# Reordering the beginning of an adaLN + attention + ReGLU kernel: the norms, the first units and idle matmuls

## The chip, the cores and the metric

The kernel runs on one core of a Trainium2 chip. The metric is the device time of one launch in microseconds (us). TensorE is called PE here, its weight loads PEld, VectorE DVE, ScalarE ACT, GpSimd POOL, and the queue that issues most DMAs SP.

## The reference

One transformer block with adaptive layer norm on 2048 tokens of width 576, in float32:

```python
mod = (_silu(c) @ w_mod).reshape(c.shape[0], 6, 1, -1)
sa, ca, ga, sb, cb, gb = (mod[:, 0], mod[:, 1], mod[:, 2], mod[:, 3], mod[:, 4], mod[:, 5])
h = _layernorm(x) * (1 + ca) + sa
x = x + ga * A(h)     # A: q = h @ wq, 32 heads of 128; 16 kv heads from a cache, the last 512 keys;
                      #    softmax(q k^T / sqrt(128)) v, then @ wo
h = _layernorm(x) * (1 + cb) + sb
x = x + gb * B(h)     # B: ((gate > 0) * gate * up) @ W_down, gate = h @ W_gate, up = h @ W_up, F = 4608
```

## The kernel before

**Numbers in two parts.** A factor of an attention product is kept as a high part rounded to fp32r and a low part, the remainder (`split`, `hi`, `lo`). A product is three matmuls: high by high, weight's low by high, weight's high by low.

**Units.** Attention is cut into 128 units. A unit is one of 32 heads with one of four blocks of 512 tokens (`qb` 0 to 3). `VIS` lists which key/value group `g` (two heads) is visited with which blocks, and `UNITS` is the flat order. In before it starts with group 0 on blocks 0, 1, 2, 3, so units 0 and 1 use block 0, units 2 and 3 block 1, 4 and 5 block 2, 6 and 7 block 3; then group 1.

**One unit on the engines** (`u` is its number). PE makes the scores (`s_half`, 12 matmuls into two PSUM tiles `s`), the projection of the next unit (`qproj`, 14 matmuls, `qps`), the value product of the previous unit (`pv_half`, 12 matmuls in two halves) and pieces of the output projection (`wo`, 12 short matmuls). DVE takes the maximum of the scores (`t`), ACT and DVE split the projection (`qhi`, `qlo`), ACT exponentiates (`p`) and rounds (`hi`), POOL adds up (`ks`) and makes the low part (`lo`). The maximum crosses partitions in one of two ways. The `by_moves` way stays on DVE (`cross`). The other uses a small PE matmul with `quad` (`qm`, in `spread`), behind the next projection in PE's order. In the first `PE0` = 4 units (`by_pe`) the maximum is also subtracted on PE (`minus`, 4 matmuls).

**The norms.** Attention needs the normalized, modulated and transposed input `hT` of a block before the first projection of that block. `LayerNorm` does it in steps: `st` (statistics of one of four token tiles, DVE), `rs` (reciprocal root, POOL), `nm` (normalize a tile, ACT), `tr` (20 transposes on PE into PSUM, `lta`), `af` (scale and shift by the modulation columns `mcol`, then high and low part). The norm of block n for attention is called `a0` to `a3`. The columns come from `mod_step` (DVE adds up rows of `w_mod` scaled by silu(c), tiles `wmb`) and `mod_col` (PE sums over partitions, `mps`). `m2` and `gate_row` do the same for the gate `ga`, which scales `wo` on DVE before it is split.

**What sets the order.** Every engine runs its instructions in the order in which the Python code writes them. The unit loop calls `run(u, k)` between its parts, which emits all steps of the list `sched` that are due at time 10*u + k. `step(name, t, fn)` puts a step there; in before, `PLAN` shifts `t` by name. Steps with negative times come ahead of unit 0. Loads of weights (`rwA` for wq, `rkv` for keys or values, `roga` for wo) go through two buffers (`raw`); a buffer is free again when its low part is made. The SP queue issues loads in order, and a load whose buffer isn't free holds up those behind it. `keep` and `again` write split weights to DRAM and fetch them back for a second visit of a group.

## Time and profile before

| | |
|---|---|
| time, median of 3 runs | 2862.01 us (2859.11 to 2862.62) |
| the profiled execution | 2857.6 us, its span 2855.8 us |
| PE busy | 2815.0 us, 99% of the span |
| DVE, POOL, ACT busy | 79%, 74%, 52% |
| mean granted PE clock | 0.998 |

The profiled execution is 4.4 us below the median of the runs, and 1.8 us of it lie outside the span. The start of a unit is taken here as the start of its first score matmul (line 496). Units 0 to 8 begin at 35.42, 46.92, 60.74, 74.21, 92.26, 106.26, 122.33, 134.73 and 146.55 us of the span. From unit 7 on a unit takes some 11.85 us.

### The profile page before, as it was taken

The numbers are of one execution on the slowest core, as the hardware profiler recorded it, in microseconds if no ns is written. First come the engines' busy times: TensorE is split into PE (matmuls) and PEld (weight loads), VectorE is DVE, ScalarE is ACT, GpSimd is POOL, SyncE is SP. The second block draws the span as 40 slices with busy tenths as digits, with TensorE's granted clock in tenths as the row PEclk, the third lists the DMA queues.
The fourth block names the chain that finished last, engine by engine and source line by source line (L and its number), as shares of the span: only waits on it lengthen the run. The fifth ranks groups of instructions, "written<-read, shape, count | busy, mean of one in ns | idle before, by whom it ended". The sixth has DMA issues, their size and how long they took to land.

```text
span 2855.8 us, 41174 instructions
## 1 busy us (share of the span) xinstructions
PE 2815.0 (99%) x15006; PEld 2449.5 (86%) x15006; DVE 2246.8 (79%) x3384; ACT 1476.7 (52%) x2105; POOL 2123.8 (74%) x1564
## 2 busy tenths in 40 slices
PE   6999999999999999999999999999999999999999
PEld 5788888888888888888888888888888888888888
DVE  7899999999889998888889756676677466666666
ACT  5766666666766666666656444444444122222221
POOL 5688888888899989877778766788777356656653
PEclk9999999999999999999999999999999999999999
DMA  4012132222232213312243456666667844444442
GB/s 163 24 45 79 65 106 85 83 82 100 95 104 94 92 62 131 105 70 80 68 155 139 150 213 229 231 240 231 234 234 261 338 165 154 155 155 159 159 154 106
DMA packets 164506, 399.57 MB, mean 140 GB/s; under 512 B 15056, under 2 KB 62160, under 8 KB 164304
## 3 DMA queue, kind: packets, MB, share of 16 engines
q1 hardware_dynamic: 132912, 284.69, 29.9%
q10 hardware_dynamic: 31392, 112.26, 10.0%
q8 instruction: 118, 1.93, 0.3%
q14 instruction: 84, 0.69, 0.1%
HBM read 271.16 MB, written 154.57 MB: 149 GB/s over the span
## 4 chain that ended last, share of the span: by engine, by line
PE 83%; DVE 6%; POOL 5%; issue 2%; ACT 2%; DMA 2%; SPq 0%; ACTq 0%; DVEq 0%; POOLq 0%
PE gu L1016 26%; PE wo L660 12%; PE qps L424 11%; PE md L660 8%; PE st_P L1118 6%; PE s L498 3%; PE s L497 3%; PE s L496 3%; PE pv L635 3%; PE pv L634 3%; PE pv L633 3%; POOL lo L600 2%; DVE t L501 1%; DVE p L591 1%; POOL wop L795 1%
## 5 line engine op out<-in xcount | busy, mean ns | idle before, releaser
L600 POOL TENSOR_TENSOR lo<-p,hi 128x1024 fp32r<-128x1024 f32 x256 | 610.6, 2406 | 1.1 <-ACT hi L577 1.1
L609 POOL TENSOR_TENSOR ks<-ks,p 128x512 f32<-128x512 f32 x256 | 351.7, 1374 | 238.7 <-DVE ks L606 135.5
L501 DVE TRANSPOSE_TENSOR_REDUCE t<-s 128x32 f32<-128x1024 f32 x256 | 313.8, 1239 | 85.9 <-PE s L498 76.6
L1016 PE MATMUL gu<-hop_B,wop 128*128 128x512 f32 x1512 | 375.0, 391 | 0.2 <-POOL wop L795 0.2
L1016 PEld LDWEIGHTS gu<-hop_B,wop 128*128 128x128 f32 x1512 | 274.9, 188 | 51.1 <-POOL wop L795 0.9
L1016 PE MATMUL gu<-hop_T,wop 128*128 128x512 f32 x1260 | 316.1, 391 | 0.0
L424 PE MATMUL qps<-hTa,wA 128*128 128x512 f32 x1288 | 312.9, 394 | 3.1 <-DVE hTa L372 1.6
L660 PE MATMUL wo<-woga,ohi 128*128 128x288 f32 x1472 | 298.8, 295 | 2.0 <-POOL woga L183 1.4
L591 DVE TENSOR_TENSOR p<-s,mb 128x1024 f32<-128x1024 f32 x246 | 290.3, 1219 | 4.2
L424 PEld LDWEIGHTS qps<-hTa,wA 128*128 128x128 f32 x1288 | 244.5, 190 | 56.6 <-DVE hTa L372 3.2
L476 ACT ACTIVATE qhi<-qps 128x512 fp32r<-128x512 f32 x128 | 76.4, 597 | 366.9 <-PE qps L424 358.4
L660 PEld LDWEIGHTS wo<-woga,ohi 128*128 128x128 f32 x1472 | 245.9, 188 | 18.8 <-POOL woga L183 3.4
L1016 PEld LDWEIGHTS gu<-hop_T,wop 128*128 128x128 f32 x1260 | 227.8, 188 | 39.0
L577 ACT CAST hi<-p 128x1024 fp32r<-128x1024 f32 x256 | 259.5, 1042 | 1.5
L660 PE MATMUL md<-wogb,hhi 128*128 128x288 f32 x1272 | 256.9, 295 | 0.4 <-DVE acc L671 0.4
L593 ACT ACTIVATE p<-p 128x1024 f32<-128x1024 f32 x246 | 249.5, 1051 | 13.7 <-DVE p L591 13.4
L671 DVE TENSOR_TENSOR acc<-md,acc 128x576 f32<-128x576 f32 x159 | 119.9, 755 | 160.4 <-PE md L660 159.8
L660 PEld LDWEIGHTS md<-wogb,hhi 128*128 128x128 f32 x1272 | 210.9, 188 | 12.6 <-DVE acc L671 1.4
L1127 DVE TENSOR_TENSOR acc<-st_P,acc 128x576 f32<-128x576 f32 x160 | 121.1, 757 | 127.9 <-PE st_P L1118 127.9
L660 PE MATMUL wo<-woga,olo 128*128 128x288 f32 x736 | 217.8, 296 | 1.3 <-POOL olo L649 1.2
L660 PE MATMUL md<-wogb,hlo 128*128 128x288 f32 x636 | 187.5, 295 | 0.0
L649 POOL TENSOR_TENSOR olo<-rb,ohi 128x512 fp32r<-128x512 f32 x128 | 167.4, 1308 | 15.2 <-ACT ohi L645 15.0
(283 smaller groups left out, 7095.3 us busy)
## 6 DMA issues: line engine op xcount, KB each, us to landing
wop<-wk_P SPq DMA_DIRECT2D x133, 640.0 KB
wk_P<-wop ACTq DMA_DIRECT2D x119, 640.0 KB
wr<-wlay SPq DMA_DIRECT2D x68, 384.0 KB
rogb<-wd SPq DMA_DIRECT2D x68, 288.0 KB
againq<-akq SPq DMA_DIRECT2D x18, 640.0 KB
rwA<-wq SPq DMA_DIRECT2D x32, 320.0 KB
wlay<-wg SPq DMA_DIRECT2D x36, 256.0 KB
roga<-wo SPq DMA_DIRECT2D x32, 288.0 KB
```

The costliest lines, as they stand in the source:

```text
L424: return [lambda i=i, a=a, b=b: nc.tensor.matmul(ps, a, b, start=(i == 0), stop=(i == n - 1)) for i, (a, b) in enumerate(ops)]
L501: nc.vector.tensor_reduce(t5[u][:, 2 * h:2 * h + 2, :].rearrange("p k b -> p (k b)"), t.rearrange("p k (b j) -> p (k b) j", j=32), axis=AX ...
L577: nc.scalar.copy(hi_[u, h], pt[u, h])
L591: nc.vector.tensor_tensor(p, t, bc[u][:, None, :].to_broadcast([P, 2, 512]), op=ALU.subtract)
L593: nc.scalar.activation(p, p, AF.Exp, bias=0.0, scale=1.0)
L600: nc.gpsimd.tensor_sub(lo_[u, h], pt[u, h], hi_[u, h].bitcast(F32))
L609: nc.gpsimd.tensor_tensor(ks_[u], ks_[u], p[:, j, :], op=ALU.add)
L649: nc.gpsimd.tensor_sub(olo[u], o.pop(u), ohi[u].bitcast(F32))
L660: nc.tensor.matmul(ps[:, half, :H2], a[:, sl], w[b][:, cs], start=(n == 0 and seed is None), stop=(n == 5), skip_group_check=seed is not None)
L1016: nc.tensor.matmul(ps, a, c, start=s not in heir(m) and i == 0 and s not in seeds_of(m), stop=i == len(ops) - 1, skip_group_check=True)
L1118: nc.tensor.matmul(ps[:, j, :H2], x[:, sl], w[:, y, :], start=n == 0 and not second, stop=n == 2, skip_group_check=True)
L1127: nc.vector.tensor_tensor(t, ps[:, :, :H2], t, op=ALU.add)
```

## The change

- **Units.** `VIS` begins with group 0 on block 0, then group 1 on blocks 0 to 3, then group 0 on blocks 1 to 3. Block 0 so serves units 0 to 3, block 1 units 4 and 5, block 2 units 6 and 7, block 3 units 8 and 9. The weights of heads 2 and 3 and of group 1 are loaded ahead; those of group 0 are kept in DRAM and fetched again.
- **First norm.** `a0` is written out by hand. Its 512-wide parts are normalized before the tails, transposes go token tile by token tile, and `finish` takes high and low parts straight from the PSUM banks in an order given by `FIN0`. The sums for the two modulation columns lose the ACT and POOL help (`pre_scale`, `pre_add`), and the last rows of column 0 are added by PE.
- **Idle matmuls.** `warm` puts 22 matmuls whose result nobody reads between the first steps of PE.
- **Where steps go.** `PLAN` holds absolute times now, for norms, gate, loads, projections and stores. The projections of units 1 to 4 are steps of their own; that of unit 2 goes ahead of that of unit 1 and to another PSUM pool. The norms 2 to 4 and `m2` are spread over units 0 to 7.
- **Small ones.** Units 4 to 7 use `qm` on PE and not `cross` on DVE (`MOVE0` = 8). The first weights get their low parts on DVE. `c` is loaded through ACT's queue.

PE's rows ahead of the first projection, in before: the sum for column 1, the first transposes of `a0` (bank `lta`), the sum for column 0 (`mps`).

```order
L171 MATMUL mps_448<-ones,wmb_4_400 128x1 x5
L329 MATMUL lta_0_483<-ident,xna_0_459 128x128
L329 MATMUL lta_0_483<-ident,xna_1_462 128x128
L329 MATMUL lta_0_483<-ident,xna_2_465 128x128
L329 MATMUL lta_0_483<-ident,xna_3_468 128x128
L329 MATMUL lta_0_483<-ident,xna_0_459 128x128
L329 MATMUL lta_0_483<-ident,xna_1_462 128x128
L329 MATMUL lta_0_483<-ident,xna_2_465 128x128
L329 MATMUL lta_0_483<-ident,xna_3_468 128x128
L171 MATMUL mps_493<-ones,wmb_4_406 128x1 x5
```

The same place on PE now, with the idle matmuls (`warm`).

```order
L1420 MATMUL warm_462<-acc_126,ident 128x128 x4
L1420 MATMUL warm_467<-wmb_0_396,ident 128x128 x4
L358 MATMUL lta_0_472<-ident,xna_0_446 128x128 x2
L1420 MATMUL warm_475<-wmb_0_396,ident 128x128 x2
L358 MATMUL lta_0_472<-ident,xna_1_449 128x128 x2
L1420 MATMUL warm_480<-wmb_0_396,ident 128x128 x2
L358 MATMUL lta_0_472<-ident,xna_2_451 128x128 x2
L1420 MATMUL warm_485<-wmb_0_396,ident 128x128 x2
L185 MATMUL mps_488<-ones,wmb_4_400 128x1 x5
L358 MATMUL lta_0_472<-ident,xna_3_453 128x128 x2
L1420 MATMUL warm_498<-wmb_0_396,ident 128x128 x8
L181 MATMUL mps_513<-sT,wmb_4_406 128x1 x4
```

The transposes now stand token by token ahead of the column sums, with idle matmuls between them.

DVE's rows between the low part of the first projection (`qlo`) and the first maximum (`t`), in before. `lfa` and `hTa` numbered 2, 3, 8 and 1 here are those of block 1.

```order
L480 SCALAR_TENSOR_TENSOR qlo_595<-qps_566,qhi_593 128x512
L387 TENSOR_SCALAR lfa_2_637<-lta_2_0_623,mcol_454,mcol_499 128x512
L387 TENSOR_SCALAR lfa_3_639<-lta_2_1_628,mcol_454,mcol_499 128x512
L391 CAST hTa_2_633<-lfa_2_637 128x512
L391 CAST hTa_3_635<-lfa_3_639 128x512
L395 TENSOR_TENSOR hTa_7_636<-lfa_3_639,hTa_3_635 128x512
L391 CAST hTa_8_650<-lfa_4_651 128x512
L387 TENSOR_SCALAR lfa_1_661<-lta_0_614,mcol_454,mcol_499 128x512
L501 TENSOR_REDUCE t_0_674<-s_0_667 128x32
L501 TENSOR_REDUCE t_0_674<-s_1_676 128x32
```

The same place on DVE now, from the last low parts of block 0.

```order
L457 TENSOR_TENSOR hTa_4_552<-lfa_0_571,hTa_0_548 128x512
L457 TENSOR_TENSOR hTa_8_556<-lfa_4_566,hTa_8_556 64x512
L457 TENSOR_TENSOR hTa_6_554<-lfa_2_562,hTa_2_550 128x512
L136 TENSOR_SCALAR wmb_4_416<-wmb_0_412,sT 128x576
L306 BN_STATS sta_1_608<-acc_127 128x6 x2
L307 BN_AGGR mva_607<-sta_1_608 128x2
L557 SCALAR_TENSOR_TENSOR qlo_614<-qps_584,qhi_612 128x512
L139 SCALAR_TENSOR_TENSOR wmb_4_416<-wmb_0_412,sT,wmb_4_416 128x576
L578 TENSOR_REDUCE t_0_628<-s_0_621 128x32
L578 TENSOR_REDUCE t_0_628<-s_1_630 128x32
```

Block 1's high and low parts are gone from this place; one statistics step and two steps of `m2` stand there.

PE's rows of unit 1 in before, from its last score matmul to the value product of unit 0 (`pv`); `qps_775` is the projection of unit 2.

```order
L498 MATMUL s_1_761<-qlo_729,kv_0_559 128x512
L424 MATMUL qps_775<-hTa_0_655,wA_471 128x512 x2
L424 MATMUL qps_775<-hTa_1_657,wA_471 128x512 x2
L424 MATMUL qps_775<-hTa_2_633,wA_471 128x512 x2
L424 MATMUL qps_775<-hTa_3_635,wA_471 128x512 x2
L424 MATMUL qps_775<-hTa_8_650,wA_471 128x512 x2
L424 MATMUL qps_775<-hTa_4_656,wA_471 128x512
L424 MATMUL qps_775<-hTa_5_658,wA_471 128x512
L424 MATMUL qps_775<-hTa_6_634,wA_471 128x512
L424 MATMUL qps_775<-hTa_7_636,wA_471 128x512
L530 MATMUL qm_769<-t_1_759,quad 128x80
L633 MATMUL pv_815<-hi_0_722,kv_1_687 128x512
```

The same place on PE now.

```order
L575 MATMUL s_1_767<-qlo_728,kv_0_529 128x512
L607 MATMUL qm_778<-t_1_765,quad 128x80
L710 MATMUL pv_811<-hi_0_709,kv_1_734 128x512
L711 MATMUL pv_811<-hi_0_709,kv_1_734 128x512
L712 MATMUL pv_811<-lo_0_749,kv_1_734 128x512
L710 MATMUL pv_811<-hi_0_709,kv_1_734 128x512
L711 MATMUL pv_811<-hi_0_709,kv_1_734 128x512
L712 MATMUL pv_811<-lo_0_749,kv_1_734 128x512
L664 MATMUL s_0_758<-mr_797,minus 128x512 x2
L664 MATMUL s_1_767<-mr_797,minus 128x512 x2
L374 MATMUL lta_0_842<-ident,xna_0_775 128x128
```

No projection stands between the scores and `qm` in unit 1 any more (that of unit 2 went into unit 0), and block 1's first transposes come here.

```diff
+PLAN = {'wq2.c': -64, 'wq3.l': -64, 'v0.l': -50, 'wq3.c': 2.2, 'k1.l': -64, 'v0.c': 6, 'k1.c': 2.2, 'x2': 2.2,
...
+WARM = (4, 4, 2, 2, 2, 0, 8, 0)
+Q0 = "h3 h0 h1 h2 l0 l3 l1 b4 l2"
+QS = 5
+QW = [2]
+QLATE = [4, 8]
+FIN0 = "f3v h3v l3p h1a f2v f1a f4a h2v h0a l1p f0a l0v h4a l4v l2v"
+MOVE0 = 8
...
-    nc.sync.dma_start(cT, c)
+    nc.scalar.dma_start(cT, c)
...
     def by_moves(u):
-        return PE0 <= u < MOVES
+        return MOVE0 <= u < MOVES
...
-    VIS = [(g, (0, 1, 2, 3)) for g in range(HKV - NLAST)]
+    VIS = [(0, (0,)), (1, (0, 1, 2, 3)), (0, (1, 2, 3))]
+    VIS += [(g, (0, 1, 2, 3)) for g in range(2, HKV - NLAST)]
...
     def step(name, t, fn, *args):
-        sched.append((t + PLAN.get(name, 0), len(sched), fn, args))
+        sched.append((PLAN.get(name, t), len(sched), fn, args))
...
+        def finish(self, plan):
...
+            for op in plan.split():
+                d, e = int(op[1]), op[2]
...
+                if op[0] == "l":
+                    eng = nc.vector if e == "v" else nc.gpsimd
+                    eng.tensor_sub(lo, fs[d][p0:], hi.bitcast(F32)[p0:])
+                    continue
+                dst, a, m = hi if op[0] == "h" else fs[d], add[:, d:d + 1], mul[:, d:d + 1]
+                if e == "v":
+                    nc.vector.tensor_scalar(dst, self.ps[d], m, a, op0=ALU.mult, op1=ALU.add)
+                else:
+                    nc.scalar.activation(dst, self.ps[d], AF.Identity, bias=a, scale=m)
...
+    def warm(k, src):
+        if WARM[k]:
+            t = psM.tile([P, 512], F32, tag="mm", name=f"warm{k}")[:, :P]
+            for _ in range(WARM[k]):
+                nc.tensor.matmul(t, ident, src, start=True, stop=True)
...
+    for i in range(4):
+        first(ln0.stats, i)
+    first(ln0.rstd)
+    first(mod_step, 1, 0, big[1, 0])
+    first(mod_step, 1, 1, big[1, 1])
+    first(ln0.shift)
+    for part in range(2):
+        for i in range(4):
+            first(ln0.norm, i, part)
...
+    first(lambda: mods.update(a=(mc[0](), mc["one"])))
+    first(ln0.trans, (2, 3), psS, "s")
+    first(ln0.trans, (4,), psW, "w")
+    first(ln0.finish, FIN0)
...
+    step("wq1.l", -70, pq1[0])
+    step("wq2.l", -70, pq2[0])
+    step("wq1.c", -66, pq1[1])
     step("q0", -65, qproj, 0, 0, 14)
...
+    for v in range(1, QS):
+        step(f"q{v}.a", 10 * v - 9, qproj, v, 0, 9)
+        step(f"q{v}.b", 10 * v - 9, qproj, v, 9, 14)
```

More of the change, by code (lines that the diff above doesn't have):

```diff
@@ L165, in mod_col @@
         m = msum[j]
-        assert steps_done[j] == (3 if j == 1 else 5)
+        assert steps_done[j] == 5 - (j == 0)
+        ps = psM.tile([P, 512], F32, tag="mm", name=f"mps{j}")
+        if j == 0:
+            w = big[0, 4]
+            for t in range(5):
+                a = w[:64, t * P:(t + 1) * P] if t < 4 else big[0, 2][:64, 2 * D:1280]
+                nc.tensor.matmul(ps[:, 8 + t:9 + t], a, sT[:64, 4:5], start=True, stop=True)
         if j < 3:
             mod_pad(j)
-        ps = psM.tile([P, 512], F32, tag="mm", name=f"mps{j}")
         for t in range(5):
@@ L1282 @@
     pk0[0]()
+    load_mod(2, "wC")
     load_x(1)
@@ L1359 @@
-    step("wq1.l", -67, pq1[0])
-    step("v0.l", -66, pv0[0])
+            if key == "a":
+                step(f"{nm}.lo{k}", 23 if t_af[k] == 20.5 else 28 if t_af[k] == 25 and qb == 1 else t_af[k] + (1 if t_af[k] % 20 == 5 else 0), lambda ds=ds: ln.rest[ds]())
+    mc = {}
+    ln0 = LayerNorm(0, "a", [(hp, "hT", 512)] * 4)
+    t = iter(range(-400, 0))
+    def warm(k, src):
[3 more added lines that the diff above has]
+                nc.tensor.matmul(t, ident, src, start=True, stop=True)
@@ new lines, in first @@
+    def first(fn, *args):
+        step("start", next(t), fn, *args)
+    for i in range(4):
[7 more added lines that the diff above has]
+            first(ln0.norm, i, part)
+    for i in range(2, 5):
+        first(mod_step, 1, i, big[1, i])
+    first(warm, 0, acc[3][:, :P])
+    first(warm, 1, big[1, 0][:, :P])
+    for i in range(3):
+        first(ln0.trans, (0, 1), psS, "s", (i,))
+        first(warm, 2 + i, big[1, 0][:, :P])
@@ new lines, with tail @@
+    first(setd(mc, 1, lambda: mod_col(1, 1.0)))
+    first(warm, 5, big[1, 0][:, :P])
+    first(ln0.trans, (0, 1), psS, "s", (3,))
+    first(warm, 6, big[1, 0][:, :P])
+    for i in range(4):
+        first(mod_step, 0, i, big[0, i])
+    first(lambda: mc.update(one=mc[1]()))
+    def tail():
+        a = big[0, 4][:64, None, 512:D]
+        nc.gpsimd.tensor_copy(big[0, 2][:64, 2 * D:1280].rearrange("p (r n) -> p r n", r=2), a.to_broadcast([64, 2, 64]))
+    first(tail)
+    first(setd(mc, 0, lambda: mod_col(0, 0.0)))
@@ L1426 @@
         seen.add(g)
-    for i in range(1, first):
+    for i in range(1, HKV - NLAST):
         B = 80 * i
```

206 lines of the change are left out of this document (129 added, 77 removed).

## The prediction

> **What bounds the kernel now.** The page's first part says which engine sets the time.
>
> ```profile
> PE 2815.0 (99%) x15006; PEld 2449.5 (86%) x15006; DVE 2246.8 (79%) x3384; ACT 1476.7 (52%) x2105; POOL 2123.8 (74%) x1564
> ```
>
> PE is busy in all but 40.8 us of the span of 2855.8, so the question is where those lie. I cut the span where the first score matmul of each unit starts and asked for busy time by window (length, PE, PEld, DVE, ACT, POOL, then granted clock, DMA share, GB/s).
>
> ```profile
> 0.00:15.17 15.17, 0.00 (x0) 0.00 (x0) 10.49 (x30) 6.88 (x11) 4.25 (x13) 1.00 0.86 310
> 15.17:35.42 20.25, 17.73 (x74) 14.73 (x75) 14.05 (x30) 10.82 (x19) 10.99 (x10) 1.00 0.73 263
> 35.42:46.92 11.50, 7.94 (x35) 5.75 (x33) 10.70 (x18) 5.37 (x9) 7.04 (x6) 0.96 0.33 104
> 46.92:60.74 13.82, 12.87 (x44) 10.22 (x45) 10.74 (x27) 5.66 (x7) 8.18 (x6) 0.79 0.08 26
> 60.74:74.21 13.47, 12.52 (x62) 9.88 (x60) 12.00 (x20) 11.98 (x19) 10.86 (x8) 1.00 0.00 1
> 74.21:92.26 18.05, 14.86 (x68) 11.65 (x67) 16.40 (x35) 11.19 (x16) 11.68 (x9) 0.91 0.06 20
> 92.26:106.26 14.00, 13.62 (x76) 11.33 (x75) 12.00 (x23) 12.23 (x20) 10.02 (x8) 1.00 0.01 2
> 106.26:122.33 16.07, 14.17 (x74) 10.86 (x72) 12.47 (x22) 10.99 (x15) 10.07 (x6) 1.00 0.13 43
> 122.33:134.73 12.40, 12.11 (x65) 10.22 (x63) 12.09 (x22) 8.71 (x12) 9.85 (x6) 1.00 0.07 23
> 134.73:146.55 11.82, 11.82 (x64) 10.24 (x63) 10.52 (x20) 8.10 (x12) 10.09 (x7) 1.00 0.16 48
> 35.42:146.55 111.13, 99.91 (x471) 80.15 (x470) 96.92 (x178) 74.23 (x104) 77.79 (x54) 0.95 0.10 31
> 146.55:2855.80 2709.25, 2697.32 (x14466) 2354.62 (x14464) 2125.30 (x3149) 1384.74 (x1973) 2030.75 (x1489) 1.00 0.41 142
> ```
>
> Rows 3 to 10 are units 0 to 7. A unit is whole at 11.82 us, where PE never idles. From 146.55 on PE idles 11.93 us in 2709, and the change leaves that stretch as it is. What can be won lies ahead of it: the first 35.42 us, then 11.2 idle us in the eight units and a slow clock (0.04 of 11.50, 0.21 of 13.82 and 0.09 of 18.05, together 5.0 us). The end moves by as much as the start of unit 8, now 146.55.
>
> The chain of waits shows what unit 0 waited for (start, length, what):
>
> ```profile
> 25.31 1.70 POOL rsa L293
> ...
> 33.20 0.61 ACT qhi L476
> 33.83 0.69 DVE qlo L480
> 34.58 1.53 DVE lfa L387 x2
> ...
> 36.82 1.66 DVE hTa L395
> ...
> 39.54 2.30 DVE t L501 x2
> ...
> 42.44 0.45 PE qm L530 x2
> ...
> 43.60 0.72 DVE mb L566
> 44.34 0.63 ACT mr L569
> ```
>
> The first maximum (`t`) waits from 34.58 to 39.54 behind DVE's work for block 1.
>
> **Part 1: the first scores, 35.42 before.** These rows of the timeline carry it.
>
> ```profile
> 1.17 1.84 SPq L108 DMA_DIRECT2D acc<-x  x4
> 4.42 0.82 DVE L285 BATCH_NORM_STATS2 sta<-acc 128x6 f32<-128x288 f32 x2 [1.22 <-DMA acc<-x]
> ...
> 8.66 0.21 DVE L286 BATCH_NORM_AGGREGATE mva<-sta 128x2 f32<-128x12 f32 x1
> ...
> 9.28 1.04 POOL L293 TENSOR_TENSOR rsa<-rsa,mhalf 128x4 f32<-128x4 f32 x1
> ...
> 15.17 2.29 PE L171 MATMUL mps<-ones,wmb 128*128 128x1 f32 x10 [15.17 <-DVE wmb L1341]
> ...
> 26.77 5.46 PE L424 MATMUL qps<-hTa,wA 128*128 128x512 f32 x12 [1.13 <-DVE hTa L391]
> ...
> 33.00 2.67 PE L329 MATMUL lta<-ident,xna 128*128 128x128 f32 x20
> ...
> 36.53 1.40 POOL L395 TENSOR_TENSOR hTa<-lfa,hTa 128x512 fp32r<-128x512 f32 x1 [0.48 <-DVE hTa L391]
> ```
>
> And these of the groups by shape in the first 140 us (count, busy us, mean ns):
>
> ```profile
> L387 DVE TENSOR_SCALAR lfa<-lta,mcol,mcol 128x512 f32<-128x512 f32 x5 | 3.8, 794 | 0.1
> ...
> L130 DVE SCALAR_TENSOR_TENSOR wmb<-wmb,sT 128x576 f32<-128x576 f32 x3 | 2.5, 819 | 0.1
> ```
>
> - `c` leaves SP's queue, so x is issued 0.45 earlier: statistics end at 8.4, not 8.87. One small DVE step, then the root on POOL, 1.04 alone or 1.70 as at 25.31 beside DVE work. DVE runs `m1` beside it now, so I take 1.70: 10.4, and 10.65 with `shift`. ACT's first tile follows at 11.5.
> - DVE goes on alone: three `m1` steps, four `m0` steps and two pads, 6 x 0.82 and small ones, to 16.7. The two low parts of weights, 1.5, lie behind that, to 18.2, while PE works.
> - PE from 11.5: 8 transposes, 14 idle matmuls and 15 column matmuls. A column sum of five took 10 instructions, so each plain fp32 matmul is two: 8 + 28 + 30 = 66 instructions. Fast, an instruction of this kind takes 0.133 (20 in 2.67 at 33.00): 8.8. Slow, 0.229 (10 in 2.29 at 15.17): 15.1. I take fast, as 8 idle matmuls stand ahead: 20.3. The remaining 12 transposes, 1.6, bring the banks to 21.6.
> - `finish`: four DVE steps of 0.79, then three low parts of 0.69 (a `qlo` is the same size). ACT's six run beside it, POOL makes two. A DVE low part took 1.66 at 36.82 while POOL ran one from 36.53 to 37.93, so these queue: 0 to 1.4, I take 0.7. Sum: 21.6 + 3.2 + 2.1 + 0.7 = 27.6, and the last matmul follows at once.
> - `qhi` 0.61 is met by PE at 28.2; one statistics step (1.03) and `m2` stand before `qlo` on DVE, so the scores run freely from 29.0. That is 6.4 earlier than 35.42. ACT casts two more weights ahead of `qhi`, due at 25.5. With all that is issued before them they make 7.6 MB by the tiles' sizes; at the 310 GB/s of the window to 15.17 that is 24.5 us, and their buffers are free at 18.2, so they cost nothing, with one microsecond to spare.
>
> The Trainium skill ("SBUF — State Buffer", section "SBUF: two separate sides") says that a DVE instruction with two SBUF inputs and a POOL instruction hold one port pair in turn, each for its whole length. By that the 0.7 would be 1.4 and the time 0.7 more; the row at 36.82 agrees with the rule.
>
> **Part 2: units 0 to 7, 111.13 before.** A unit's work by rows of the chain:
>
> ```profile
> 58.60 0.93 PE s L587 x4
> ...
> 63.91 0.97 PE mps L151 x4
> ...
> 125.81 3.17 PE qps L424 x14
> 128.98 1.58 PE wo L660 x12
> ...
> 130.79 0.23 PE pv L634
> ```
>
> Twelve score or value matmuls are 2.73.
>
> - Unit 0, 11.50 before: 2.3 of scores, two projections 6.3, `qm` 0.45, `minus` 0.93. The maximum no longer waits for block 1, and its chain (2.30, 0.5, a statistics step, 0.45, 0.72, 0.63) lies under the projections: 10.1.
> - Unit 1, 13.82 before: scores 2.73, `qm`, value product 2.73, `minus`, 16 transposes 2.1, gate sum 0.97: 9.9. No projection covers the maximum any more: from the scores' end 2.30 + 0.5 + 0.7 for the sums + 0.45 + a statistics step 1.03 + 0.3 + 0.72 + 0.63, 6.6, against which only half a value product stands (and its low part waits for POOL, which has `ks` and a value split ahead). Then come half of `minus` 0.5, ACT's exponential 1.0 (it frees the score bank that the transposes need), 8 transposes 1.05, the other half of the value product 1.4, the gate sum 1.0, ACT's copy of it 0.8 and 8 transposes 1.05: 16.1, of it some 6 of waits. A slow clock can follow such a pause, as in before's row 46.92:60.74 (2.9 us): 0 to 2.9, I take 1.0. 17.1.
> - Unit 2, 13.47 before: 10.5 of work; its second score bank waits 1.4 for block 1's low parts on DVE, `qlo` another 1.0: 13.0.
> - Unit 3, 18.05 before: 11.6 and 1.1 behind ACT's exponentials: 12.7. Before waited here for block 2's high and low parts on DVE and ACT.
> - Units 4 and 6, 14.00 and 12.40 before: 11.85 + 20 transposes 2.67 + `qm` 0.45 each: 15.0.
> - Units 5 and 7, 16.07 and 11.82 before: 11.85 + 0.45 + 1.0, as the projection's last low parts come behind the maximum (2.30) on DVE: 13.3.
>
> Sum: 10.1 + 17.1 + 13.0 + 12.7 + 15.0 + 13.3 + 15.0 + 13.3 = 109.5, 1.6 less than 111.13. The norms' work moves into units that were full, so most of the second part is an exchange.
>
> Edits costed at nothing: the stores of group 0 (issued by ACT, hidden by its idle half), fetching it back from unit 7 on (three units ahead), POOL's tail copy (under `m0`). Without cover a store's issue costs a few tenths on ACT.
>
> **Sum.** 6.4 + 1.6 = 8.0: 2857.6 becomes 2849.6. The runs' median stands 4.4 above the profiled execution, so 2854.0 there.
>
> **The rivals.**
> - *PE stays slow until the first projection.* The 66 instructions take 15.1, not 8.8, and 12 transposes 1.2 more: 7.5 later, 0.5 left: 2861.5. For it: in before PE was nearly unbroken from 15.17, with transposes and column sums, and still took 0.455 a projection matmul (12 in 5.46 at 26.77, against 14 in 3.17). Against: the idle matmuls stream 128 columns each, more than a column sum. It decides if PE isn't fast by about 16 us. The Trainium skill ("TensorE: Matmul & The Clock Gate", section "Part 1: The HAM clock gate (the "warmup" mystery)") says that some 3.4 us of sustained activity open the clock. By that before would have been fast by 20, and the row at 26.77 doesn't show it; with it this rival falls and my sum stands. Chance 0.15.
> - *It comes out slower: ACT stands behind a store.* The split of the fourth query weight (`wq3`) takes the buffer of the first, which ACT's own queue is storing to DRAM; ACT's cast waits for that store, and behind it stand the key cast and unit 0's `mr`, due near 36. Landing by 35 costs nothing, each us later is one us; landing 22 us after its issue at 29 loses 16, the 8.0 and 8.0 more: 2870. Against: the loads ahead are small and the row 35.42:46.92 moves only 104 GB/s. Chance 0.08.
> - *Waits of units 1 and 2 are shorter and nothing collides at the start*: first scores run freely from 27, units 1 and 2 take 3 us less: 13 us, 2849. For it: DVE's statistics steps in unit 1's chain (1.03 each) can fall into time in which DVE waits for PE, and I added each in full. Against: the sums over `p` and the value split queue on POOL in the same stretch. Chance 0.20.
>
> **How the numbers follow.** My forecast has 0.57, and holds 2850 to 2859 (its unknowns: 1.4 at the port, 2.9 of clock, 1 to 2 of waits). 0.2% is 5.7 us, about what a measurement of this kernel can tell from no change. Faster by that means below 2856.3: 0.47 of the forecast's 0.57 and the third rival's 0.20, 0.67. Same: 0.10 of the forecast, 0.13 of the slow clock, 0.02 of the store, 0.25. Slower: 0.02 of the slow clock, 0.06 of the store, 0.08. The range reaches from 2845 (the third rival with 4 us more) to 2861, the greater part of the slow clock's case left out.
>
> **What would show it.** Right: scores of unit 0 between 27 and 30; transposes at 0.13 from 12 on; PE idle some 6 us in unit 1; units 4 and 6 near 15; unit 8 near 139. Wrong: instructions of 0.23 between 12 and 20; ACT idle ahead of the cast of `wA` behind a DMA; unit 8 after 146; a unit after the eighth that differs from 11.85.

## The result and the profile after

The changed kernel takes 2866.96 us (median of 21 runs, 2861.68 to 2872.55) against 2858.44 for the kernel before (21 runs, 2855.06 to 2862.62): 1.0029 times as long, 95% interval 1.0022 to 1.0035. The forecast was 8.0 us faster; it is 8.5 slower. The profiled execution took 2869.27 us, 11.7 above that of before, its span 2867.5. Before's median over 21 runs lies 0.8 above its profiled execution, not 4.4 as over the three runs that the forecast had; the forecast difference of 8.0 doesn't hang on that.

The first part of the changed kernel's page, busy time by engine:

```profile
PE 2822.0 (98%) x15068; PEld 2453.9 (86%) x15068; DVE 2262.1 (79%) x3380; ACT 1473.9 (51%) x2099; POOL 2109.9 (74%) x1554
```

Busy time by window in the changed kernel, cut at the first score matmul of units 0 to 8 and of unit 127, the last one (columns as in the prediction):

```profile
0.00:28.68 28.68, 17.50 (x109) 14.63 (x109) 22.36 (x50) 13.47 (x21) 6.78 (x13) 1.00 0.96 317
28.68:41.11 12.43, 11.09 (x46) 8.36 (x47) 11.40 (x25) 3.94 (x6) 5.39 (x5) 1.00 0.66 231
41.11:62.38 21.27, 14.55 (x51) 9.75 (x50) 19.66 (x37) 13.81 (x22) 15.46 (x12) 0.76 0.18 59
62.38:75.44 13.06, 10.91 (x52) 8.51 (x51) 12.89 (x22) 7.74 (x12) 8.23 (x8) 1.00 0.13 35
75.44:90.98 15.54, 12.32 (x58) 9.38 (x56) 14.33 (x23) 8.85 (x13) 10.33 (x7) 1.00 0.20 70
90.98:105.85 14.87, 14.44 (x87) 12.60 (x85) 13.73 (x22) 13.14 (x20) 12.32 (x8) 1.00 0.51 179
105.85:119.20 13.35, 12.83 (x67) 10.41 (x66) 12.65 (x21) 9.01 (x14) 9.33 (x9) 1.00 0.20 72
119.20:135.31 16.11, 14.64 (x86) 12.59 (x85) 13.23 (x21) 13.86 (x20) 12.17 (x8) 1.00 0.00 1
135.31:148.27 12.96, 12.42 (x67) 10.54 (x66) 12.09 (x20) 7.29 (x10) 4.98 (x3) 1.00 0.18 54
148.27:1581.18 1432.91, 1427.29 (x7482) 1236.50 (x7481) 1295.99 (x2171) 953.53 (x1302) 1202.87 (x739) 1.00 0.29 93
1581.18:2867.50 1286.32, 1273.97 (x6986) 1120.59 (x6984) 833.80 (x979) 429.30 (x667) 822.07 (x747) 1.00 0.57 197
```

The same last two stretches in the kernel before:

```profile
146.56:1579.87 1433.31, 1427.32 (x7482) 1236.50 (x7481) 1296.94 (x2171) 955.71 (x1307) 1207.81 (x742) 1.00 0.28 92
1579.87:2855.80 1275.93, 1269.99 (x6986) 1118.11 (x6984) 828.35 (x980) 429.02 (x667) 822.93 (x747) 1.00 0.56 199
```

Unit 0 begins at 28.68, 6.7 earlier than before and nearly where the forecast had it. The eight units then take 119.6, where the forecast had 109.5 and before 111.1, so unit 8 begins at 148.27, 1.7 later than before. (Executions of one and the same program text differ here too: in `b_swap` and `b_noS3`, which are the kernel before as far as unit 127, unit 8 begins at 146.98 and 147.86.) Units 8 to 126 are alike (1432.91 against 1433.31). The stretch from unit 127 to the end, with the last unit and the MLP, takes 10.4 longer, with the same number of PE instructions: PE idles 12.35 in place of 5.94 and is busy 4.0 longer. There are two places to explain, then: units 0 to 3, and that last stretch. Unit 8 was forecast at 138.5, so 9.7 of the profiled execution's miss lie ahead of it, and 10.4 behind the start of unit 127.

**Units 0 to 3.** The chain of waits of the changed kernel in unit 1 (start, length, what):

```profile
49.40 0.06 DVE rr L641
49.48 2.29 DVE rr L642
51.80 0.72 DVE mb L643
52.55 0.63 ACT mr L646
53.22 1.24 PE s L664 x2
```

And POOL's timeline at that place:

```profile
47.05 4.69 POOL L677 TENSOR_TENSOR lo<-p,hi 128x1024 fp32r<-128x1024 f32 x2
```

`rr` splits a 128x16 column of maxima into two parts so that PE can subtract it (`minus`). Its second step takes 2.29 and ends when POOL's two `lo` end, at 51.74. All instructions that write `rr`, by line (count, ns min/median/max, first and last start), in the changed kernel:

```profile
L641 DVE CAST rr<-t x5: 121/546/1285, 36.2 to 1588.1; 128x16 fp32r<-128x16 f32 x5
L642 DVE TENSOR_TENSOR rr<-t,rr x5: 176/177/2311, 37.3 to 1589.4; 128x16 fp32r<-128x16 f32 x5
```

and in the kernel before:

```profile
L564 DVE CAST rr<-qm x5: 113/114/176, 43.2 to 1586.9; 128x16 fp32r<-128x16 f32 x5
L565 DVE TENSOR_TENSOR rr<-qm,rr x5: 174/174/175, 43.4 to 1587.0; 128x16 fp32r<-128x16 f32 x5
```

The input is `t` now, a tile in SBUF, where it was `qm`, a bank of PSUM. That comes from one line of `max_bc` that neither my excerpt of the diff nor my list of costs had:

```diff
-        r = bps[u][:, 256:272] if by_pe(u) else t5[u][:, 0, :]
+        r = t5[u][:, 0, :]
```

It holds for the units in which PE subtracts the maximum: 0 to 3, and the last one, 127, where the cast took 1.28 for 0.11.

PE's wait isn't all of it. The granted clock in the changed kernel's unit 1 is 0.76 over 21.27, 5.1 us lost by the forecast's way of counting. With the old line (`a_psum` below) it is 0.90, 1.7 lost; PE idles 1.6 less in that unit and is busy 2.6 less, with the same instructions:

```profile
42.99:60.07 17.08, 11.95 (x51) 8.21 (x50) 16.33 (x36) 13.76 (x22) 13.10 (x11) 0.90 0.20 65
```

**The last stretch.** DVE's timeline in the MLP of the changed kernel:

```profile
1911.29 6.07 DVE L900 TENSOR_TENSOR wr<-wr,wr 128x768 f32<-128x768 f32 x1
1917.28 0.75 DVE L748 TENSOR_TENSOR acc<-md,acc 128x576 f32<-128x576 f32 x1
```

POOL's at the same time:

```profile
1910.99 0.97 POOL L871 TENSOR_TENSOR wop<-wr,wop 32x256 fp32r<-32x256 f32 x1 [1.83 <-ACT wop L870]
1911.93 1.29 POOL L872 TENSOR_TENSOR wop<-wr,wop 128x512 fp32r<-128x512 f32 x1
1913.19 1.43 POOL L201 TENSOR_TENSOR wogb<-rogb,wogb 128x576 fp32r<-128x576 f32 x1
1914.58 1.28 POOL L1233 TENSOR_TENSOR hlo<-c,hhi 128x512 fp32r<-128x512 f32 x1
1915.83 0.71 POOL L871 TENSOR_TENSOR wop<-wr,wop 32x256 fp32r<-32x256 f32 x1
1916.51 1.97 POOL L872 TENSOR_TENSOR wop<-wr,wop 128x512 fp32r<-128x512 f32 x1
```

And PE's:

```profile
1918.08 0.53 PE L737 MATMUL md<-wogb,hhi 128*128 128x288 f32 x2 [2.41 <-DVE acc L748]
```

`wr<-wr,wr` is one of four sums of weight tiles that DVE makes for the MLP; the code calls it `S3`. It begins at 1911.29, when POOL has just begun a row of instructions without a gap, and it ends 0.8 after the fifth of them, at 1917.36; the sixth takes 1.97 where its like took 1.29. Behind `S3` on DVE stands `acc`, which empties the bank of the down projection that PE wants next: PE waits 2.41. `S3` is made 17 times. In the changed kernel 15 of these take some 0.95 and two 6.07 and 6.08 (at 1911.29 and 1985.71); in the kernel before none:

```profile
L823 DVE TENSOR_TENSOR wr<-wr,wr x17: 944/947/953, 1621.4 to 2191.9; 128x768 f32<-128x768 f32 x17
```

```profile
L900 DVE TENSOR_TENSOR wr<-wr,wr x17: 944/947/6080, 1625.0 to 2203.1; 128x768 f32<-128x768 f32 x17
```

No line of that code is changed. What is changed is when DVE and POOL come there relative to each other: in the kernel before POOL runs nothing when `S3` begins, 17 times out of 17.

The 4.0 by which PE is busy longer are in the main a slow clock again, 3.0 more lost than in before. There are two such stretches, one behind the last unit's `rr` and one behind the first long `S3`; behind the second long one the clock stays at 1.00:

```profile
1591.80:1595.30 3.50, 3.50 (x15) 3.23 (x14) 1.29 (x2) 3.44 (x5) 1.31 (x2) 0.51 0.02 6
1919.50:1923.00 3.50, 3.50 (x12) 2.83 (x11) 0.76 (x1) 0.83 (x1) 3.06 (x3) 0.51 0.95 335
```

With 4.9 more of waits for `acc`, 0.9 for `mr` in the last unit and 0.6 for a late weight, that makes 9.4 of the 10.4.

### The profile page after: what moved, and what is told of

It reads as the page before. It is cut to its first block, busy times and chain, and to the rows that moved or that the text cites. A ratio compares the mean times of both kernels' runs of the same rounds, so it can differ in the third digit from the quotient of the medians.

```text
span 2867.5 us, 41282 instructions
## 1 busy us (share of the span) xinstructions
PE 2822.0 (98%) x15068; PEld 2453.9 (86%) x15068; DVE 2262.1 (79%) x3380; ACT 1473.9 (51%) x2099; POOL 2109.9 (74%) x1554
## 4 chain that ended last, share of the span: by engine, by line
PE 81%; DVE 6%; POOL 6%; DMA 3%; ACT 2%; issue 2%; SPq 0%; ACTq 0%; POOLq 0%; DVEq 0%
PE gu L1093 24%; PE wo L737 12%; PE qps L499 11%; PE md L737 6%; PE st_P L1195 6%; PE s L575 3%; PE s L574 3%; PE s L573 3%; PE pv L712 3%; PE pv L711 3%; PE pv L710 3%; POOL lo L677 2%; POOL wop L872 1%; DVE t L578 1%; DVE ws L900 1%
## 5 line engine op out<-in xcount | busy, mean ns | idle before, releaser
L499 PE MATMUL qps<-hTa,wA 128*128 128x512 f32 x1190 | 284.4, 389 | 0.5 <-DVE hTa L417 0.5
L737 PE MATMUL wo<-woga,ohi 128*128 128x288 f32 x1376 | 279.7, 295 | 1.1 <-POOL woga L201 0.7
L499 PEld LDWEIGHTS qps<-hTa,wA 128*128 128x128 f32 x1190 | 223.2, 188 | 47.3 <-DVE hTa L417 0.9
L737 PEld LDWEIGHTS wo<-woga,ohi 128*128 128x128 f32 x1376 | 229.8, 188 | 16.1 <-POOL woga L201 2.9
L737 PE MATMUL wo<-woga,olo 128*128 128x288 f32 x688 | 203.6, 296 | 1.3 <-POOL olo L726 1.0
```

The costliest lines, as they stand in the source:

```text
L499: return [lambda i=i, a=a, b=b: nc.tensor.matmul(ps, a, b, start=(i == 0), stop=(i == n - 1)) for i, (a, b) in enumerate(ops)]
L737: nc.tensor.matmul(ps[:, half, :H2], a[:, sl], w[b][:, cs], start=(n == 0 and seed is None), stop=(n == 5), skip_group_check=seed is not None)
```

## The experiments

Sixteen kernels; "a" stands on the changed kernel, "b" on the kernel before. All times are medians, with the ratio to the kernel before in the same measurement (its median in brackets). Unit 8, unit 127 and the rest from there come from the profiled execution, as does the number of `S3` that took over 5 us; "rest" is the stretch from unit 127 to the end.

| kernel | us (before) | ratio, 95% | unit 8 | unit 127 | rest | long `S3` |
|---|---|---|---|---|---|---|
| before | 2858.44 | | 146.56 | 1579.87 | 1275.93 | 0 |
| after | 2866.96 (2858.44) | 1.0029, 1.0022 to 1.0035 | 148.27 | 1581.18 | 1286.32 | 2 |
| a_last | 2863.38 (2858.96) | 1.0016, 1.0007 to 1.0025 | 148.16 | 1580.82 | 1277.28 | 0 |
| a_psum | 2857.36 (2858.96) | 0.9995, 0.9986 to 1.0003 | 143.38 | 1576.05 | 1280.55 | 1 |
| b_last | 2860.93 (2858.96) | 1.0007, 0.9998 to 1.0016 | 147.77 | 1580.60 | 1278.5 | 0 |
| b_sbuf | 2862.12 (2858.96) | 1.0014, 1.0005 to 1.0023 | 150.56 | 1583.66 | 1279.9 | 1 |
| a_late | 2859.01 (2859.12) | 1.0001, 0.9992 to 1.0009 | 144.95 | 1577.89 | 1280.1 | 1 |
| a_nowarm | 2861.14 (2859.12) | 1.0008, 0.9999 to 1.0017 | 145.17 | 1578.01 | 1281.6 | 2 |
| a_both | 2857.41 (2859.24) | 0.9990, 0.9981 to 0.9999 | 141.97 | 1574.60 | 1281.80 | 1 |
| b_start | 2866.32 (2859.24) | 1.0027, 1.0016 to 1.0038 | 148.63 | 1581.79 | 1282.3 | 1 |
| a_swap | 2872.76 (2859.12) | 1.0048, 1.0036 to 1.0061 | 144.62 | 1577.06 | 1293.9 | 4 |
| b_swap | 2873.24 (2859.12) | 1.0053, 1.0041 to 1.0066 | 146.98 | 1579.90 | 1291.1 | 5 |
| a_c | 2859.06 (2858.39) | 0.9999, 0.9990 to 1.0008 | 139.69 | 1571.81 | 1287.19 | 2 |
| b_cq | 2861.26 (2858.39) | 1.0008, 0.9999 to 1.0018 | 148.10 | 1581.1 | 1279.2 | 1 |
| a_noS3 | 2852.41 (2859.21) | 0.9978, 0.9969 to 0.9986 | 141.38 | 1574.25 | 1277.15 | left out |
| b_noS3 | 2857.69 (2859.21) | 0.9999, 0.9991 to 1.0008 | 147.86 | 1580.62 | 1276.28 | left out |
| a_s3late | 2855.30 (2859.21) | 0.9988, 0.9979 to 0.9997 | 140.47 | 1573.19 | 1279.31 | 0 |
| a_s3early | 2859.42 (2859.21) | 1.0004, 0.9995 to 1.0012 | 140.42 | 1573.77 | 1284.7 | 2 |

### The column of maxima

The theory: the one line costs what is missing in units 0 to 3 and part of the end. The rival: the moved steps themselves cost it, and the place of the column is nothing. `a_psum` puts the old line back, `a_last` only for the last unit; `b_sbuf` puts the new line into the kernel before, `b_last` only for the last unit.

```diff
 a_psum:
-        r = t5[u][:, 0, :]
+        r = bps[u][:, 256:272] if by_pe(u) else t5[u][:, 0, :]
 a_last: the same with "if u == NU - 1"
 b_sbuf:
-        r = bps[u][:, 256:272] if by_pe(u) else t5[u][:, 0, :]
+        r = t5[u][:, 0, :]
 b_last: the old line with "if u < PE0"
```

> The changed kernel with the column in PSUM in units 0 to 3 and in 127, the old line. Port theory: in unit 1 the subtraction into rr, 2.28 us beside POOL's lo, takes 0.2; the pause on PE shortens by 2.1 us and the slow clock behind it by some tenths to 2 us, so unit 8 starts 2 to 4 us earlier than 148.27 and the median lies 2 to 4 us under a_last's. Rival: something else ends as late in unit 1 (the low parts on POOL), unit 8 starts within 0.5 us of 148.3 and the median equals a_last's.

> The changed kernel, but in the last attention unit (127) the column of maxima stays in PSUM as in before. Port theory: the cast to rr there, 128x16, took 1.28 us against 0.11 because its input now lies in SBUF and POOL runs lo beside it; it comes back to 0.11 and the start of the MLP stage moves from +3.5 to about +1.3 us. Carry-over theory: the 8 us lost later in the MLP stage (two weight sums held 6.1 us each) follow from that late start, so the median falls to 2857 to 2861. Rival, independent: the MLP stage loses its 8 us whatever the last unit does, and only 2.2 us go: about 2864.7.

> The kernel before with the column in SBUF in units 0 to 3 and in 127. Port theory: units 0 to 3 lose 0 to 4 us beside b_last, wherever POOL happens to run at the rr steps, rr steps over 0.5 us show it. Rival: the same time as b_last, since the projection covers the step in these units.

> The kernel before, with only the last unit's column of maxima in SBUF. Port theory: the cast to rr of unit 127 takes some 1.2 us, and the MLP stage starts about 2.2 us later. Carry-over theory: the MLP stage loses 5 to 8 us more, median 2865 to 2868. Independent: 2.2 us alone, about 2860.6.

The instructions that write `rr` in `a_psum`, by line:

```profile
L641 DVE CAST rr<-qm x5: 111/113/174, 38.4 to 1583.0; 128x16 fp32r<-128x16 f32 x5
L642 DVE TENSOR_TENSOR rr<-qm,rr x5: 174/174/176, 38.6 to 1583.2; 128x16 fp32r<-128x16 f32 x5
```

The waits are gone from all five units, and the median falls by 9.6 against the changed kernel's (0.0034 of the ratio). `a_last` alone gains 3.6, which leaves the other 6.0 for units 0 to 3. `a_last`'s profiled execution, 2859.88, is the lowest of its 11 runs, so its rest of 1277.28 is better than its usual one. In the kernel before the same line costs 3.2 (`b_sbuf`) and 2.0 for the last unit alone, whose interval includes no change. It costs in units 0 to 3 there too: PE waits 6.4 for `mr` in `b_sbuf` and 2.1 in `b_last`, and unit 8 begins 2.8 later. That the old order feels it less because a projection covers the chain, where in the new order none does in unit 1, is an argument, not shown. Nor does the late start of the MLP by itself bring the hold of `S3`, as the expectations for `a_last` and `b_last` had it: `b_last` has the late start and no hold, and its 2860.93 is what the loss in the last unit alone was to give. The line is the larger part of the miss, 9.6 of 16.5. With the old line the change isn't slower any more, but it isn't measurably faster either, though unit 127 begins 3.8 earlier than in before.

### The start

Two questions were open: whether the idle matmuls do what the forecast took them to do, and why `a_psum` begins unit 0 at 30.56. Up to there it is the same program as the changed kernel, and so are `a_last` and `a_swap`; their profiled executions begin unit 0 at 28.68 (changed kernel), 28.72, 30.56 and 31.78. `a_nowarm` is `a_psum` without idle matmuls; `a_late` is `a_psum` with two weights split later; `a_both` is `a_late` with eight more idle matmuls; `b_start` is the kernel before with the changed kernel's first norm and idle matmuls alone.

```diff
 a_nowarm: -WARM = (4, 4, 2, 2, 2, 0, 8, 0)
           +WARM = (0, 0, 0, 0, 0, 0, 0, 0)
 a_late:   (the times of two steps)
           -'wq1.c': -66   ... 'wq2.c': -64
           +'wq1.c': -62.8 ... 'wq2.c': -62.6
 a_both:   a_late, and
           -WARM = (4, 4, 2, 2, 2, 0, 8, 0)
           +WARM = (4, 8, 2, 2, 2, 0, 8, 0, 4)
           +    first(warm, 8, acc[3][:, :P])      # ahead of ln0.finish
```

> a_psum without the 22 idle matmuls. If the idle matmuls made PE fast, transposes and column sums take 0.23 an instruction and projection matmuls 0.45: the prediction's first rival, worth up to 7.5 us at unit 0, less what DVE and ACT hide; unit 0 begins 2 to 6 us later. If PE is fast anyway, unit 0 begins within 1 us of 28.7 to 30.6.

> a_psum, but the splits of the second and third query weight (wq1, wq2) come behind the split of unit 0's projection. In a_psum the DVE low parts of the first block (hTa) stood beside POOL's low parts of these weights, PE idled 0.7, 1.1 and 1.2 us inside the first projection, its clock was granted at 0.50 until 34, and unit 0 began at 30.56. Port theory: without that neighbour the low parts take some 0.7 each, the clock stays at 1.00, unit 0 begins at 26.5 to 28 and the scores run freely from 28 to 29; unit 8 starts 2 to 4 us earlier than a_psum's 143.38, of which the later weights may take back 1. Rival: POOL's low parts only move into unit 0, where qlo or the projection of unit 2 waits for them; unit 8 within 1 us of a_psum's, same median (2857.4).

> a_late with more idle matmuls: 8 in place of 4 in the second group, so that PE does not pause ahead of the first transposes (it paused 1.3 us at 10.5 in a_psum and a_late, and ran the transposes at 0.23 an instruction in a_late), and 4 more between the last transposes and the first projection. If the late start of unit 0 in a_late (30.61) was the slow PE, instructions take 0.13 from 12 on and the projection 0.23, unit 0 begins at 27 to 28.5, unit 8 at 140.5 to 142.5, median 2853 to 2856. Rival: the weights that are split later hold the projection of unit 2, and unit 8 stays at 143.4 or later: 2857 or more.

> The kernel before with one part of the change alone: the first norm written out by hand with its idle matmuls, c on ACT's queue, the old column in PSUM; units, projections and the other norms in before's order, block 1's statistics in DVE's pause ahead of the second column sum. If the start is what the change wins, the first block is ready 4 to 6 us earlier, unit 0 begins near 30 to 32, but its first maximum still waits for block 1 on DVE, so unit 8 begins at 142 to 145 and the median is 2854 to 2857, as good as a_psum: the new order of the units then wins nothing by itself. Rival: block 1's norm is late on ACT and PE stands with its transposes ahead of the scores; unit 8 at 147 or later, no gain without the new order.

The second column sum in PE's timeline, in the changed kernel:

```profile
14.09 1.25 PE L185 MATMUL mps<-ones,wmb 128*128 128x1 f32 x10
```

and in `a_nowarm`, with the window around it:

```profile
13.56 2.29 PE L185 MATMUL mps<-ones,wmb 128*128 128x1 f32 x10
...
12.00:22.00 10.00, 9.97 (x45) 8.68 (x44) 6.49 (x13) 5.27 (x11) 0.46 (x1) 1.00 1.04 340
```

Without idle matmuls an instruction takes 0.229 in place of 0.125, although PE works through the window without a pause; unit 0 begins at 32.51. The granted clock reads 1.00 there all the same, so here the durations show a slow PE that the column doesn't. In `a_psum` the clock falls back later:

```profile
23.38 5.65 DVE L457 TENSOR_TENSOR hTa<-lfa,hTa 128x512 fp32r<-128x512 f32 x3
...
24.97 3.51 POOL L201 TENSOR_TENSOR wA<-rwA,wA 128x640 fp32r<-128x640 f32 x2 [0.47 <-ACT wA L200]
...
28.00:34.00 6.00, 4.23 (x9) 3.01 (x10) 4.28 (x8) 0.60 (x1) 0.48 (x1) 0.50 0.85 297
```

Its three DVE low parts meet two weight splits on POOL and take 5.65 where the changed kernel's took 3.12; PE stands, then runs at 0.50 from 28 to 34. `a_late` moves the splits away (3.10 for the three), and its unit 0 is still not early: PE paused 1.34 at 10.5 and then took over 0.2 an instruction until 15.7, and later the granted clock was 0.50 for 6.9 us from 22.5 on, so that the projection took 5.91. Its median is 1.7 above `a_psum`'s. `a_both` has more idle matmuls at both places, and its first score matmul stands where the forecast had it (27.87 to 28.14 in the four kernels with this start):

```profile
28.14 0.50 PE L573 MATMUL s<-qhi,kv 128*128 128x512 f32 x1 [0.69 <-ACT qhi L553]
```

Yet `a_both`'s median is that of `a_psum`, with unit 127 now 5.3 earlier than in before and a rest of 1281.80. And the new start without the new unit order is a loss of 7.1: in `b_start` the second block's transposes stand ahead of unit 0 on PE and wait for ACT, and unit 0 begins at 37.66:

```profile
34.30 3.71 PE L374 MATMUL lta<-ident,xna 128*128 128x128 f32 x17 [0.76 <-ACT xna L343]
```

### The MLP

Theories for the rest: (1) the hold of DVE's `S3` by POOL; (2) transfers that lie at another place in a queue (`c`, and a shorter last piece of `w_mod`); (3) the four sums together stand badly in DVE's order. For (3), `a_swap` (on `a_psum`) and `b_swap` move all sums and the work for the next weights behind the down projection's piece. For (2), `a_c` (on `a_both`) takes the old transfers, `b_cq` puts the new ones into the kernel before. For (1), `S3` is left out. The last two are `a_both` with only `S3` moved, behind `acc` or one slot earlier.

```diff
 a_swap, b_swap:
-                if (m or i) and not early:
-                    sums(m, i)
-                    others(m, i)
...                        # md.pop(0)(), the down projection's piece
+                if (m or i) and not early:
+                    sums(m, i)
+                    others(m, i)
 a_c:      -nc.scalar.dma_start(cT, c)    +nc.sync.dma_start(cT, c)    (and whole pieces of w_mod)
 b_cq:     the reverse
 a_noS3, b_noS3:
-        ... 2: [(0, "S4")], 5: [(1, "S3")], 6: [(1, "S2")]
+        ... 2: [(0, "S4")], 6: [(1, "S2")]
 a_s3late: sums(m, 5) behind md.pop(0)()
 a_s3early: sums(m, 5) at the end of slot 4
```

> a_psum, but in the MLP stage the sums over two weights (wr, ws, DVE, two inputs in SBUF) are written behind the addition of the down piece (acc) and no longer ahead of it. In a_psum at 1903.60 such a sum took 6.05 us beside an unbroken row of POOL work and acc behind it held up PE, 3.8 us of the span. Port theory: a held sum no longer holds acc; the stage from unit 127 to the end falls from 1280.6 to about 1275 to 1277, median 2852 to 2855. Rival: the sum is held all the same and the split that needs it is late, or another DVE step is caught instead; median within 1.5 us of 2857.4.

> The kernel before with the same exchange of the sum and the addition. Port theory: before's profile shows no 6 us hold and loses 0.4 us there, but its runs spread from 2854.6 to 2863.9; if that spread is this hold, the median falls by 1 to 3 us and the highest runs go. Rival: the spread has another source and the median stays within 1 us of 2858.9.

> a_both with the transfers of the start as in before: c on SP's queue, the last piece of the modulation weights loaded with all 128 rows. a_both's unit 127 began 5.3 us before before's (1574.6 against 1579.9), but it lost that again behind 1574: 1281.8 to the end against 1275.9. In the MLP stage the load of hx_T waits for the store of hb, 1.3 us in before and its variants, 3.1 to 3.5 in five of the eight others. If the place of transfers in the queues sets this (two queues are shifted by one transfer each), the stage falls back to 1276 to 1279, and the median to 2852 to 2855. Rival: the stage's holds follow from when its steps meet, whatever the queues: stage 1280 to 1283, median 2857 to 2858, at most 0.5 later from the start.

> The kernel before with only these two transfers as the change has them. If their place in the queues matters, the load of hx_T waits over 3 us for the store, the stage from unit 127 on takes 1280 or more and the median is 2861 to 2864. Rival: within 1 us of before's 2859, stage at 1276 to 1279.

> a_both without the weight sum S3 (17 DVE steps of the MLP stage; its work is left out). If the held sum is what eats the gain, the additions are never late, the stage from unit 127 on takes 1274 to 1277 (1281.8 in a_both) and the median is 2850 to 2853. Rival: another DVE step is caught in its place, as c was in before (3.8 us); stage within 1.5 us of a_both's, median above 2856.

> The kernel before without S3 in the same way. Its profile shows no held S3 and 0.4 us of waits for the addition, so if the theory holds it gains 0 to 2 us (2857 to 2859), and a_noS3 lies 4 to 6 us below it. If b_noS3 gains as much as a_noS3, the sum costs both the same and the difference between the kernels has another cause.

> a_both with S3 alone behind the addition in its slot; the other three sums stay. If the sum is the cause and can wait, the stage takes 1275 to 1279, median 2851 to 2855. Rival: a later S3 pushes S2 and the weight splits behind it, as in a_swap; PE waits for POOL's split and the median is 2860 or more.

> a_both with S3 at the end of the slot before. If it finds POOL's pause or at least no addition behind it there, stage 1275 to 1279, median 2851 to 2855. Rival: it waits for its transfer or for POOL there and holds the next addition instead; median 2857 or more.

**(3) falls.** Both swaps cost 14 to 15 us. What is put off there is wanted soon: in that stage of `a_swap` PE waits 15 times, 7.4 us in total, for POOL's part of the next weights (`wop`). As the swap moves more than the sums, it says nothing of a smaller move.

**(2) isn't borne out.** `b_cq` stands 2.9 above before, with an interval that just includes no change, and one long `S3` can account for as much. `a_c` has the old transfers and gains nothing at the end: it begins unit 8 at 139.69 and unit 127 eight us ahead of before, and has the longest rest but for `a_swap` and `b_swap`. A late weight has a part in that: PE waits 2.9 for a `wop` from DRAM, where eleven of the other kernels wait 0.3 to 1.3 for one, and before not at all.

**(1) holds.** The waits of PE for `acc` in that stage (us in total, times, longest), in the changed kernel, in the kernel before, in `a_c` and in `a_noS3`:

```profile
PE md L737 <- DVE acc L748: 5.3, 4, 2.4
```

```profile
PE md L660 <- DVE acc L671: 0.4, 1, 0.4
```

```profile
PE md L737 <- DVE acc L748: 4.8, 2, 2.4
```

```profile
PE md L737 <- DVE acc L748: 0.3, 1, 0.3
```

Over all kernels that make `S3` in its usual place, it takes 0.95 or 6.05 and more, with nothing between, at the passes near 1905 and 1980 of the span (in `b_start` once, 7.27, at 2156.68). Sorted by the number of long ones, with `a_s3early` beside them, the rest takes 1275.9, 1277.3 and 1278.5 with none, 1279.2 to 1282.3 with one, and 1281.6, 1284.7, 1286.3 and 1287.2 with two. The means are 1277.2, 1280.6 and 1285.0, so one is worth some 3 to 4 us; each is one execution. What one costs has two parts. PE waits some 2.4 for `acc` (3.6 behind the 7.27), and behind 9 of these 14 long ones the granted clock is 0.50 for some 3.5 us, 1.7 lost. That, the column in the last unit and the late `wop` are why the numbers within a group lie apart: `b_last`, with no long one, has the wait for `mr` (0.9) and one such stretch of slow clock (1.7) in its 1278.5. Without `S3` the rest is alike on both sides, in `a_noS3`

```profile
1574.25:2851.40 1277.15, 1270.31 (x6986) 1118.15 (x6984) 805.31 (x963) 428.75 (x667) 823.65 (x747) 1.00 0.58 198
```

1277.15, where `a_both`, the same kernel with it, had

```profile
1574.60:2856.40 1281.80, 1272.30 (x6986) 1119.02 (x6984) 831.74 (x979) 429.09 (x667) 822.69 (x747) 1.00 0.57 198
```

and in `b_noS3` 1276.28. On the medians leaving it out is worth 5.0 to `a_both` and 1.5 to the kernel before, whose interval includes no change. The 3.5 between is an estimate of what the hold costs the reordered kernel beyond what it costs before; by the spread of the runs its size is uncertain by about as much as itself. (Both kernels leave that sum out of the weights, so their results lack it.)

`a_s3late` keeps the sum but puts it where no `acc` stands behind it. Its longest is 4.18, and PE waits for `acc` little:

```profile
PE md L737 <- DVE acc L748: 1.8, 4, 0.8
```

It takes 2855.30, ratio 0.9988 (0.9979 to 0.9997), below both kernels and the lowest median of those that leave nothing out, though its interval and that of `a_both` overlap almost wholly. `a_s3early` only moves the meeting: two long ones, 4.8 us of waits.

**Left open.** Why the clock falls behind some of these pauses and not behind others is open: the two waits of 2.41 in the changed kernel are alike, and only the first is followed by 0.50. So is what sets the wait for the `wop` from DRAM, 0.3 to 2.9. The load of `hx_T`, which the expectation for `a_c` names, has no part in it: in no kernel does PE show a wait for it in that stage.

## Why the prediction was wrong, point by point

- **The step that failed first: the list of edits costed at nothing.** It left out the edit to `max_bc`, which moves an operand of a small DVE instruction from PSUM to SBUF. It costs 9.6, more than the 8.5 by which the kernel is slower. The forecast for unit 1 itself allowed 0.7 for the sums over `p` and named POOL's low parts in that stage, so the wait could have been priced: some 2.4, the length of a `lo`, for a step that meets one (2.6 for both steps together in unit 3). The slow clock behind it couldn't be read off that way; the forecast took 1.0 for unit 1, with 2.9 as its end, and in the changed kernel it was 5.1.
- **The second: "the change leaves that stretch as it is".** True of units 8 to 126 (0.4 apart), false of what follows. The last unit has the same edited line, and the MLP, whose code stands as it was, depends on when DVE and POOL reach it. `a_psum` was 3.8 ahead at unit 127 and 1.6 at the median, `a_c` 8.1 ahead at unit 127 and 0.7 behind at the median. "The end moves by as much as the start of unit 8" was the assumption; the runs show it doesn't.
- **The lengths of units 0 to 7** were nearly right where only the order decides. With the old line (`a_psum`) they are 12.43, 17.08, 12.56, 13.14, 15.04, 13.50, 16.13 and 12.94, forecast 10.1, 17.1, 13.0, 12.7, 15.0, 13.3, 15.0 and 13.3. Mis-sized are unit 0 by 2.3 and unit 6 by 1.1. Unit 0's maximum does lie under the projections: PE never idles there, and the granted clock is 0.84:

```profile
30.56:42.99 12.43, 12.43 (x47) 9.84 (x47) 9.83 (x22) 3.66 (x6) 4.07 (x4) 0.84 0.53 166
```

That is 2.0 lost to the clock. (The forecast also counts unit 0 from where the scores run freely, 0.8 behind its first score.) In the changed kernel unit 0 took the same 12.43 for another reason, a wait of 1.32 for `qlo` after the second score matmul, and in `a_both` 11.75 with one of 0.67 for POOL's low part of a weight. Unit 1's 17.08 for 17.1 is in part luck: PE idles 5.1 where the forecast had some 6, and the clock takes 1.7 where it had 1.0. In the changed kernel unit 1 took 21.27 and unit 3 15.54, the column's 4.2 and 2.4.
- **Part 1** held for the first score: 28.68 for 28.2 in the changed kernel, 28.14 in `a_both`. (Its sum has a slip: 20.3 and 1.6 are 21.9, not 21.6.) The gain of 6.4 was counted from 29.0, though, where the scores were to run freely. In the changed kernel they wait 1.32 for `qlo` and run freely from 30.73, in `a_both` from 28.91; and two further executions of the same start began only at 30.56 and 31.78, so that the early one is in part luck. The collision at `finish` was taken as 0.7, with 1.4 as its end: three low parts took 3.12, 1.0 over the forecast's 2.1, and 5.65 in `a_psum`, 3.6 over. The end was too near, as one POOL instruction per DVE instruction was counted. The Trainium skill ("SBUF — State Buffer", section "SBUF: two separate sides") says that of a DVE instruction with two SBUF inputs and a POOL instruction that reads SBUF, the one that starts first holds a shared port pair for its whole length and blocks the other. The traces agree that `rr` is held until a `lo` ends (2.29), and they go further: `S3` wasn't served after the instruction that was running, but after the fifth, 6.07 later.
- **The rivals.** The slow start fell: 0.125 an instruction from 14.09 on, and `a_nowarm` shows that the idle matmuls do it (0.229 without). With them it still came in part in `a_late` and `a_swap`, where PE paused 1.34 and 1.42 behind the first idle matmuls and was slow until about 15. By the Trainium skill's rule ("TensorE: Matmul & The Clock Gate", section "Part 1: The HAM clock gate (the "warmup" mystery)"), sustained activity of some 3.4 us opens the clock; `a_nowarm` doesn't bear that out for a row that is mostly one-column sums, since PE worked without a pause from 12 to 22 and its column sums stayed at 0.229. ACT did stand as the second rival said, but within its bound ("landing by 35 costs nothing"). ACT's timeline of the changed kernel:

```profile
33.62 0.73 ACT L200 CAST wA<-rwA 128x640 fp32r<-128x640 f32 x1 [4.99 <-DMA rwA<-wq]
...
38.26 0.62 ACT L646 CAST mr<-mb 128x512 fp32r<-128x512 f32 x1 [2.93 <-DVE mb L643]
```

It waits 4.99 for the weight, goes on at 33.6, and then has 2.93 to spare before unit 0's `mr`. Shorter waits in units 1 and 2 didn't happen either: unit 1 has its 17.1 with the old line. The result is slower by a mechanism that stood among none of them.

## What to carry to other kernels

Price every edit that moves an operand between PSUM and SBUF, however small the tile: what it costs is POOL's row of work beside it, not its own length, and then the slow clock that can follow PE's pause. A gain at the beginning reaches the end only if later meetings of DVE and POOL come out as before; look for DVE instructions that stand between POOL's rows and a PSUM bank that PE waits for, and put the bank's instruction first. When a change moves the time against its own trace, cut the span into stretches that the change didn't touch and compare those too.
